# Attention and Mish layer on one core: the scores of pairs 12 to 47 from diagonal steps to side-by-side steps, in seven PSUM banks

## The chip, the core and the metric

The kernel runs on one core of a Trainium2 chip. The core has five engines that run side by side and meet only at semaphores: PE (matrix products, with a weight load, PEld, ahead of each), DVE (vector operations), ACT (activation functions), POOL (further element-wise work) and SP (which here only issues DMAs). PE writes its results to PSUM, eight banks of 128 partitions by 512 fp32 numbers; DVE and ACT read them from there. The metric is the device time of one execution in microseconds (us); lower is better.

## What is computed

For 8 batches of 12 heads, 448 positions and a head dimension of 64, attention with an extra term in the denominator; then, over the 3584 rows of 768 numbers that come out, a layer with Mish between two products (`moe_w_in` is 768 x 2048, `moe_w_out` 2048 x 768).

```python
scores = scale * np.matmul(q, k.transpose(0, 1, 3, 2))
m = np.max(scores, axis=-1, keepdims=True)
e = np.exp(scores - m)
attn = e / (np.sum(e, axis=-1, keepdims=True) + np.exp(-m) + 1e-09)
attn_out = np.matmul(attn, v)
x = attn_out.transpose(0, 2, 1, 3).reshape(B * S, H * D)
h = x @ w_in
sp = np.where(h > 20.0, h, np.log1p(np.exp(np.minimum(h, 20.0))))
out = (h * np.tanh(sp)) @ w_out
```

## The kernel before

Two heads make a **pair**, with their 64-row halves of q and k stacked on 128 partitions; there are 48 pairs, 6 to a batch. Three pairs make a **unit** (`UNIT_PAIRS`), two units a batch. The first six pairs run in a head loop of their own (L548); from unit 2 on, one loop (L575) does for each unit u two stages, one after the other:

- The **step stage** (loop over n, L586): 12 steps, four per pair. A step is one [128 query rows] x [448 keys] block for each of two heads; the fourth step of a pair is one block only, 64 rows of each head. For a step, PE computes scores (`scores`), DVE takes the negated row maxima (L293) and ACT the exponentials with row sums (`exps`, L306). Between the steps stands the other product, `mm2_part`: gT times w_out for rows of a batch that was finished earlier, accumulated over 16 matmuls of 384 columns (a half part) or 192 (a quarter part), in chunks of two matmuls; the list `plan` says which parts run in which unit, 7 quarters in each, 5 in unit 4, the first that has any. When a part is complete, DVE copies it to SBUF (L459) and SP stores it when its row block is complete. `av_pair` (L382) multiplies the transposed exponentials with v, for the pairs of the unit before, into a bank from which DVE casts to xT (L391).
- The **w_in stage** (loop over f, L626): `mm1_mish` eight times, six matmuls of 448 columns each (L406), then ACT's Mish (L412). Between them PE transposes q and k of the next three pairs (L193, at f 1, 3 and 5), `evac_qk` scales q into qT (DVE) and copies k (ACT), and the exponentials of the unit are normalised (two pairs on DVE, L341, the third on POOL, L339) and transposed by DMA on SP's queue (L345). At f 7 the first three steps of the next unit's scores are issued. Mish and exponential use different tables on ACT, so a table is loaded at both ends of the stage; the dummy activation of L649 loads the second ahead of need.

The order on every engine is that of the program (`tc.manual_schedule`); an instruction that waits holds up everything behind it on its engine. `flush_late` issues the copies out of PSUM that earlier calls left in `late`.

PSUM before: three tiles `sc0` to `sc2` of two banks each, used as a ring by step number, and two banks `mo0` and `mo1`, handed out and returned through `mo_free`. Up to three steps are in flight; each step's scores go to PE right behind the step whose exponentials free a tile (`scores_ahead`).

How the scores are formed, from pair 12 (`DIAG_FROM`) on: the first pair of a unit is done side by side, two matmuls that each use 64 of PE's 128 rows (L272, L275), and its fourth step as one full matmul with a block-diagonal q of 64 + 64 rows (`q_rest`, L280). The second and third pair are **diagonal** (`is_diag`): `evac_qk` writes q in seven blocks of 64 rows per head with zeros between (`q_diag`, two scalings L227), and each of the seven blocks is one full 128-row matmul (L266), two per step. `av_pair` of the unit before stands ahead of the fourth step of each pair, in the unused second bank of that step's tile (`av_with`). `gather_mid` (L422) copies, after the second unit of a batch, the 64 rows that are left over at a batch border.

Of the kernel before, what the change touches and what calls it, by code (L numbers as in the profile page):

```python
# [10 lines left out]
BF16 = mybir.dt.bfloat16  # L11
AF = mybir.ActivationFunctionType
ALU = mybir.AluOpType
# [6 lines left out]
def kernel(  # L20
# [70 lines left out]
    for t_ in en_bufs:  # L91
# [10 lines left out]
    def is_diag(p):  # L102
        return p >= DIAG_FROM and p % UNIT_PAIRS > 0

    q_rest = singles.tile([128, 2, 64], BF16)
    nc.gpsimd.memset(q_rest, 0.0)

    loaded, casted, qkT, att, xT, gT, o_sbs, stats = {}, {}, {}, {}, {}, {}, {}, {}
    av_with, mids = {}, {}
    late = deque()  # L110

    def flush_late():
# [88 lines left out]
    def evac_qk(p, act=False):  # L201
        if p >= N_PAIRS:
            return
        (q_ps, k_ps), own = qkT[p]
        mo_free.extend(own)
        qd = q_diag[p % 3]
        kT = qk_pool.tile([128, S], BF16, tag="kT", name="kT")
        if not is_diag(p):
            qT = qd.rearrange("d i h r -> d (i h r)")[:, 0:S]
            qkT[p] = (qT, kT)  # L210
            if act:
                nc.scalar.mul(qT, q_ps[:, 0:S], SCALE)
            else:
                nc.vector.tensor_scalar(
                    out=qT, in0=q_ps[:, 0:S], scalar1=SCALE, scalar2=None, op0=ALU.mult
                )
            if p >= DIAG_FROM:
                nc.gpsimd.tensor_copy(out=q_rest[0:64, 0, :], in_=qT[0:64, 384:S])
                nc.gpsimd.tensor_copy(out=q_rest[64:128, 1, :], in_=qT[64:128, 0:64])
        else:  # L220
            qkT[p] = (qd, kT)
            if p < DIAG_FROM + 3:
                nc.vector.memset(qd[0:64, :, 1, :], 0.0)
                nc.vector.memset(qd[64:128, :, 0, :], 0.0)
            for h in range(2):
                rows = slice(64 * h, 64 * h + 64)
                nc.vector.tensor_scalar(  # L227
                    out=qd[rows, :, h, :],
                    in0=q_ps[rows, 0:S].rearrange("d (i r) -> d i r", i=QB),
                    scalar1=SCALE, scalar2=None, op0=ALU.mult,  # L230
                )
# [14 lines left out]
    def scores(idx):  # L246

        p, s = divmod(idx, STEPS)
        if s == 0:
            if p < HP or p % UNIT_PAIRS == 0:  # L250
                for nm in ("negm", "sums", "expm", "den", "rden"):
                    stats[nm] = st_pool.tile([128, UNIT_PAIRS, NTILE], FP32, tag=nm, name=nm)
            at = 0 if p < HP else p % UNIT_PAIRS
            att[p] = {nm: t[:, at, :] for nm, t in stats.items()}
            att[p].update(en=en_bufs[p % N_EN], whole=dict(stats))
        st = att[p]
        qT, kT = qkT[p]
        kA, kB = kT[0:64, :], kT[64:128, :]
        sc = sc_tiles[idx % len(sc_tiles)]
        if s == STEPS - 1 and p in av_with:  # L260
            av_pair(av_with.pop(p), bank=sc[:, 1, :])
        if is_diag(p):
            cols = tuple(range(2 * s, min(2 * s + 2, NTILE)))
            negm = st["negm"][:, cols[0] : cols[-1] + 1]
            for bk, i in enumerate(cols):
                nc.tensor.matmul(  # L266
                    sc[:, bk, 0:S], lhsT=qT[:, i].rearrange("d h r -> d (h r)"), rhs=kT,
                    start=True, stop=True,
                )
        elif s < 3:  # L270
            qa, qb = 128 * s, 64 + 128 * s
            nc.tensor.matmul(  # L272
                sc[:, 0, 0:S], lhsT=qT[0:64, qa : qa + 128], rhs=kA, start=True, stop=True
            )
            nc.tensor.matmul(  # L275
                sc[:, 1, 0:S], lhsT=qT[64:128, qb : qb + 128], rhs=kB, start=True, stop=True
            )
            cols, negm = (s, 4 + s), st["negm"][:, s : s + 5 : 4]
        elif p >= DIAG_FROM:
            nc.tensor.matmul(  # L280
                sc[:, 0, 0:S], lhsT=q_rest.rearrange("d h r -> d (h r)"), rhs=kT,
                start=True, stop=True,
            )
# [9 lines left out]
        nc.vector.tensor_reduce(  # L293
            out=negm, in_=sc[:, 0 : len(cols), 0:S], axis=AX.X, op=ALU.max, negate=True
        )
        st["sc", s] = (sc, cols)
# [71 lines left out]
    def av_pair(p, act=False, bank=None):  # L368
# [5 lines left out]
        av = mo_take() if bank is None else bank  # L374
        for j in range(NT):
            for h in range(2):
                if is_diag(p):
                    by_h = eT[0:SP_, j, :].rearrange("c (i h r) -> c h i r", h=2, r=64)
                    e_h = by_h[:, h]
                else:  # L380
                    e_h = eT[0:SP_, j, h * S : (h + 1) * S]
                nc.tensor.matmul(  # L382
                    av[h * 64 : (h + 1) * 64, 0:S],
                    lhsT=v_bf[:, h, j * D : (j + 1) * D],
                    rhs=e_h,
                    start=(j == 0), stop=(j == NT - 1),
                )
# [8 lines left out]
        del att[p], casted[p], qkT[p]  # L396


    def mm1_mish(b, ff):
# [3 lines left out]
        spare = ff % FF_U == 1  # L403
        h_ps = sc_tiles[0][:, 0, :] if spare else mo_take()
        for dm in range(DM_T):
            nc.tensor.matmul(  # L406
                h_ps[:, 0:S],
                lhsT=w_in_sb[:, dm, ff * 128 : (ff + 1) * 128],
                rhs=xT[b][:, dm, :],
                start=(dm == 0), stop=(dm == DM_T - 1),  # L410
            )
        nc.scalar.activation(out=gT[b][:, ff, :], in_=h_ps[:, 0:S], func=AF.Mish)  # L412
        if not spare:
            mo_free.append(h_ps)

    def gather_mid(b):
# [75 lines left out]
    plan = {}  # L492
    for g in range(B // 2):
        u0 = first_mm2 + 4 * g
        rest = plan.pop(u0, [])
        if g == 0:
            plan[u0] = [(0, i, 0, 2) for i in range(2)] + [(0, 2, 0, 1)]
            plan[u0 + 1] = [(0, 2, 1, 1)] + [(0, i, 2, 2) for i in range(3)]
# [11 lines left out]
    weight = [5.2] + [1.0] * (steps - STEPS) + [0.4] * (STEPS - 1)  # L510

    BY_POOL = 4
    LEAD = UNIT_PAIRS + 1
# [61 lines left out]
    for u in range(UNITS_PER_B, N_UNITS + 2 * UNITS_PER_B):  # L575
# [6 lines left out]
        if attn and u >= first_mm2:  # L582
            av_with.update({p0 + i: p0 + i - UNIT_PAIRS for i in range(UNIT_PAIRS)})
        end = min((u + 1) * UNIT_PAIRS, N_PAIRS) * STEPS

        for n in range(steps):  # L586
# [3 lines left out]
            if late_tp:  # L590
                transpose_pair(p0 + 2)
            exps(idx)
            if late_tp:
                evac_qk(p0 + 2)
            if u == UNITS_PER_B + 1:
# [27 lines left out]
        b, w = (u - UNITS_PER_B) // UNITS_PER_B, u % UNITS_PER_B  # L623
        nxt = p0 + UNIT_PAIRS
        todo = sorted(range(p0, nxt), key=lambda p: p in BY_PE)
        for f in range(FF_U):  # L626
            if moe:
                mm1_mish(b, w * FF_U + f)
            if u == UNITS_PER_B and f in (2, 6):
                load_w(1)  # L630
            if not attn:
# [7 lines left out]
            if nxt < DIAG_FROM and f in (4, 6):  # L639
                scores_ahead(nxt * STEPS + f // 2 - 1)  # L640
            if f == FF_U - 1:
                scores_ahead(min(nxt * STEPS + 3, N_PAIRS * STEPS))
            if f == 3:
                normalise(todo[1], dma=todo[1] not in BY_PE)
            if f == 4:
# [2 lines left out]

            nc.scalar.activation(out=one, in_=zero, func=AF.Exp)  # L649
        if moe and w == UNITS_PER_B - 1:  # L650
            gather_mid(b)
    flush_late()
    assert not pieces and all(have == 4 for _, have in o_sbs.values())

# [29 lines left out]
```

## Time and profile before

| | us |
|---|---|
| median of three runs | 481.56 (480.86 to 481.75) |
| the profiled execution | 479.95 |
| span of its instructions | 478.0 |
| w_in stage of unit 4 begins (first L406) | 117.73 |
| w_in stage of unit 9 begins | 248.63 |
| w_in stage of unit 10 begins | 274.62 |
| w_in stage of unit 15 begins | 404.79 |

The profiled execution's 479.95 us has the span of 478.0 in it and 1.95 around it. From unit 5 on a unit takes 26.0 us (26.16 in units 8 and 12, 26.66 in unit 6). The span falls into a head (to about 92 us), the units, and a tail from 407 on in which only the two products are left. Four rows of the second part of the page:

```profile
DVE  4888987968787886878687878788787869420021
ACT  5979678878787888979787878888897978412300
POOL 4877809255514334353535242433535340300000
PEclk9998798899999999999999999999999999999999
```

Each digit is the busy share of a fortieth of the span in tenths; in the last row it is the granted PE clock. Times of instructions in the text are from the span's start.

### The profile page before, as it was taken

How to read it: one execution, taken by the hardware profiler on the slowest of the kernel's cores; microseconds unless marked ns; L12 is line 12 of the kernel's file. 1: busy time of each engine (PE TensorE's matmuls, PEld its weight loads, DVE VectorE, ACT ScalarE, POOL GpSimd, SP SyncE). 2: the span in 40 equal slices, each digit the busy share in tenths (PEclk: the TensorE clock that was granted, in tenths of full speed). 3: DMA queues.
4: the chain of work that ended last, by engine and by line, in shares of the span. 5: the costliest groups of instructions: out<-in, count | busy, mean ns of one | idle time of the engine just before them, and what ended most of it. 6: DMA issues, size and time to landing. Idle time of an engine off the chain costs nothing.

```text
span 478.0 us, 8924 instructions
## 1 busy us (share of the span) xinstructions
PE 443.1 (93%) x3064; PEld 248.6 (52%) x3064; DVE 339.1 (71%) x680; ACT 350.0 (73%) x919; POOL 181.1 (38%) x315
## 2 busy tenths in 40 slices
PE   4565888898999999999999999999999999999997
PEld 2233544454655555555555555556555555556565
DVE  4888987968787886878687878788787869420021
ACT  5979678878787888979787878888897978412300
POOL 4877809255514334353535242433535340300000
PEclk9998798899999999999999999999999999999999
DMA  8999969999999989899999999899989595870113
GB/s 228 220 233 220 235 100 234 162 187 238 207 217 276 206 212 219 213 203 246 193 250 182 225 167 228 211 207 234 201 233 212 156 178 127 135 164 24 43 28 105
DMA packets 202381, 90.37 MB, mean 189 GB/s; under 512 B 159072, under 2 KB 198880, under 8 KB 202336
## 3 DMA queue, kind: packets, MB, share of 16 engines
q1 hardware_dynamic: 194848, 83.51, 81.3%
q0 software_dynamic: 7488, 6.29, 8.6%
q8 instruction: 24, 0.39, 0.3%
q14 instruction: 21, 0.17, 0.1%
HBM read 45.61 MB, written 11.01 MB: 118 GB/s over the span
## 4 chain that ended last, share of the span: by engine, by line
PE 76%; ACT 10%; DVE 9%; issue 2%; DMA 1%; POOL 0%; SPq 0%; DVEq 0%; ACTq 0%; POOLq 0%
PE mo L472 26%; PE mo L406 25%; ACT en L306 9%; PE sc L382 6%; DVE negm L293 6%; PE sc L266 5%; PE sc L406 4%; PE sc L193 3%; PE sc L272 2%; PE mo L356 1%; PE mo L382 1%; DVE en L341 1%; PE sc L280 1%; DVE eT L360 1%; DMA k_f<-in_k_dram 1%
## 5 line engine op out<-in xcount | busy, mean ns | idle before, releaser
L306 ACT ACTIVATE en<-sc,negm 128x448 bf16<-128x448 f32 x336 | 209.6, 637 | 26.4 <-DVE xT L391 10.4
L293 DVE TENSOR_REDUCE negm<-sc 128x2 f32<-128x896 f32 x192 | 180.7, 968 | 55.8 <-PE sc L275 26.0
L472 PE MATMUL mo<-w_out_sb,gT 128*128 128x384 bf16 (+1 forms) x912 | 142.3, 301 | 0.0
L406 PE MATMUL mo<-xT,w_in_sb 128*128 128x448 bf16 x672 | 137.7, 353 | 0.6 <-DVE xT L391 0.6
L412 ACT ACTIVATE gT<-mo 128x448 bf16<-128x448 f32 x112 | 61.3, 547 | 68.2 <-PE mo L406 68.1
L472 PEld LDWEIGHTS <-gT 128*128 128x128 bf16 x912 | 84.1, 98 | 48.2 <-issue 5.7
L339 POOL TENSOR_SCALAR en<-en,rden 128x448 bf16<-128x448 bf16 x122 | 76.4, 646 | 80.7 <-DVE rden L331 76.9
L406 PEld LDWEIGHTS <-w_in_sb 128*128 128x128 bf16 x768 | 72.9, 98 | 64.0 <-issue 3.0
L306 ACT ACTIVATION_READ_ACCUMULATOR en<-sc,negm 128x1 f32 x336 | 69.3, 206 | 0.0
L175 POOL CAST q_bf<-q_f 112x512 bf16<-112x512 f32 x47 | 29.0, 617 | 98.4 <-DMA q_f<-in_q_dram 98.0
L341 DVE TENSOR_SCALAR en<-en,rden 128x448 bf16<-128x448 bf16 x214 | 58.6, 345 | 0.9
L459 DVE COPY o_sb<-mo 128x384 f32<-128x384 f32 (+1 forms) x65 | 32.2, 495 | 35.1 <-PE mo L472 34.8
L266 PE MATMUL sc<-kT,qd 128*128 128x448 bf16 x168 | 47.7, 354 | 0.3 <-ACT en L306 0.2
L272 PE MATMUL sc<-kT,qd 64*128 64x448 bf16 x72 | 25.1, 411 | 12.7 <-ACT en L306 11.1
L382 PE MATMUL sc<-eT,v_bf 112*64 112x448 bf16 x288 | 34.1, 357 | 1.9 <-ACT en L306 1.7
L162 POOL CAST v_bf<-v_f 112x512 bf16<-112x512 f32 x48 | 29.5, 616 | 9.7 <-DMA v_f<-in_v_dram 8.8
L382 PEld LDWEIGHTS <-v_bf 112*64 112x64 bf16 x384 | 21.0, 112 | 22.8 <-issue 13.6
L176 POOL CAST k_bf<-k_f 112x512 bf16<-112x512 f32 x47 | 28.9, 616 | 7.5 <-DMA k_f<-in_k_dram 7.0
L227 DVE TENSOR_SCALAR qd<-sc 64x448 bf16<-64x448 bf16 x48 | 18.7, 389 | 11.9 <-PE sc L193 11.2
L266 PEld LDWEIGHTS <-qd 128*128 128x128 bf16 x168 | 16.3, 97 | 18.0 <-issue 9.2
L275 PE MATMUL sc<-kT,qd 64*128 64x448 bf16 x72 | 25.4, 415 | 0.0
L472 PE MATMUL mo<-w_out_sb,mid 128*128 128x384 bf16 x128 | 24.9, 326 | 0.0
(57 smaller groups left out, 340.1 us busy)
## 6 DMA issues: line engine op xcount, KB each, us to landing
q_f<-in_q_dram SPq DMA_DIRECT2D x48, 224.0 KB, 5.1
k_f<-in_k_dram SPq DMA_DIRECT2D x48, 224.0 KB, 5.4
v_f<-in_v_dram SPq DMA_DIRECT2D x48, 224.0 KB, 5.7
w_in_sb<-in_moe_w_in_dram POOLq DMA_DIRECT2D x12, 256.0 KB, 6.1
w_out_sb<-in_moe_w_out_dram POOLq DMA_DIRECT2D x8, 384.0 KB, 7.6
out_dram<-o_sb SPq DMA_DIRECT2D x7, 336.0 KB, 3.3
out_dram<-o_sb SPq DMA_DIRECT2D x8, 288.0 KB, 4.6
out_dram<-o_sb SPq DMA_DIRECT2D x8, 240.0 KB, 2.9
```

Source lines behind the costliest of these rows:

```text
L162: nc.gpsimd.tensor_copy(out=casted[p][2], in_=loaded.pop(p)[2])
L266: nc.tensor.matmul(sc[:, bk, 0:S], lhsT=qT[:, i].rearrange("d h r -> d (h r)"), rhs=kT, start=True, stop=True,)
L272: nc.tensor.matmul(sc[:, 0, 0:S], lhsT=qT[0:64, qa : qa + 128], rhs=kA, start=True, stop=True)
L293: nc.vector.tensor_reduce(out=negm, in_=sc[:, 0 : len(cols), 0:S], axis=AX.X, op=ALU.max, negate=True)
L306: nc.scalar.activation(out=st["en"][:, :, c, 0:SP_], in_=sc[:, bk, 0:S].rearrange("q (j c) -> q j c", j=NT), func=AF.Exp, bias=st["negm"][ ...
L339: nc.gpsimd.tensor_scalar(scalar2=1.0, op0=ALU.mult, op1=ALU.mult, **args)
L341: nc.vector.tensor_scalar(scalar2=None, op0=ALU.mult, **args)
L382: nc.tensor.matmul(av[h * 64 : (h + 1) * 64, 0:S], lhsT=v_bf[:, h, j * D : (j + 1) * D], rhs=e_h, start=(j == 0), stop=(j == NT - 1),)
L406: nc.tensor.matmul(h_ps[:, 0:S], lhsT=w_in_sb[:, dm, ff * 128 : (ff + 1) * 128], rhs=xT[b][:, dm, :], start=(dm == 0), stop=(dm == DM_T - 1),)
L412: nc.scalar.activation(out=gT[b][:, ff, :], in_=h_ps[:, 0:S], func=AF.Mish)
L459: nc.vector.tensor_copy(out=o_sb[:, cols], in_=st["o"][:, 0:n_cols])
L472: nc.tensor.matmul(st["o"][:, 0:n_cols], lhsT=src[:, ff, c0 : c0 + 128], rhs=w_out_sb[:, ff, cols], start=(ff == 0), stop=(ff == FF_T - 1),)
```

## The change

From pair 12 on (`GROUP_FROM`):

- All three pairs of a unit form their scores side by side; `q_diag`, its zeros and its pairs of scalings go. Each pair has its own `q_rest` block (`q_rests`), filled by POOL for all three.
- The ring goes. Step s of a pair has a fixed place: steps 0 to 2 in sc0 to sc2, step 3 in `mo1` (`last_sc`). `mo1` leaves `mo_free`, so that the w_out product has `mo0` alone.
- The order of the step stage is written out (`GROUPED`, one list for even and one for odd units): after the exponentials of step n, so many chunks of the product, the scores of the steps named, or an `av_pair`. Scores of a pair's fourth step and of the next pair's first two are issued together; the third step of a pair goes by itself, ahead of an `av_pair` in most places. `av_pair` uses mo1, or in odd units for the third pair a bank of sc0.
- `plan` is re-cut so that each unit has four parts: half, half, quarter, half.
- The w_in stage takes its banks in a fixed order from sc0, mo0 and mo1 (`MISH_BANK`), and `gather_mid` moves to f 6 of the next unit.

The tail and the units before unit 4 keep their order but for `plan` and `gather_mid`.

```diff
-    QB = S // 64
-    DIAG_FROM = 2 * HP
-    q_diag = [
-        singles.tile([128, QB, 2, 64], BF16, tag=f"qd{i}", name=f"qd{i}") for i in range(3)
+    GROUP_FROM = 2 * HP
+    last_sc = mo_tiles[1].rearrange("p (o n) -> p o n", o=1)
+    q_rests = [
+        singles.tile([128, 2, 64], BF16, tag=f"qr{i}", name=f"qr{i}") for i in range(UNIT_PAIRS)
     ]
...
+        if p >= GROUP_FROM:
+            q_rest = q_rests[p % UNIT_PAIRS]
+            nc.gpsimd.tensor_copy(out=q_rest[0:64, 0, :], in_=qT[0:64, 384:S])
+            nc.gpsimd.tensor_copy(out=q_rest[64:128, 1, :], in_=qT[64:128, 0:64])
...
-        if s == STEPS - 1 and p in av_with:
-            av_pair(av_with.pop(p), bank=sc[:, 1, :])
-        if is_diag(p):
-            cols = tuple(range(2 * s, min(2 * s + 2, NTILE)))
-            negm = st["negm"][:, cols[0] : cols[-1] + 1]
-            for bk, i in enumerate(cols):
-                nc.tensor.matmul(
-                    sc[:, bk, 0:S], lhsT=qT[:, i].rearrange("d h r -> d (h r)"), rhs=kT,
-                    start=True, stop=True,
-                )
-        elif s < 3:
+        if p >= GROUP_FROM:
+            sc = sc_tiles[s] if s < len(sc_tiles) else last_sc
+        if s < 3:
...
         else:
-            plan[u0] = rest + whole(g, 0) + [(g, 1, 0, 1)]
-            plan[u0 + 1] = [(g, 1, 1, 1), (g, 1, 2, 2)] + whole(g, 2)
-        plan[u0 + 2] = [(g, 4, 0, 2), (g, 4, 2, 1)] + whole(g, 3)
-        plan[u0 + 3] = [(g, 4, 3, 1)] + whole(g, 5) + [(g, 6, 0, 2)]
+            plan[u0] = plan.pop(u0) + [(g, 0, 0, 2), (g, 1, 0, 1), (g, 0, 2, 2)]
+            plan[u0 + 1] = [(g, 1, 2, 2), (g, 2, 0, 2), (g, 1, 1, 1), (g, 2, 2, 2)]
+        plan[u0 + 2] = [(g, 4, 0, 2), (g, 4, 2, 2), (g, 5, 0, 1), (g, 5, 1, 2)]
+        plan[u0 + 3] = [(g, 3, 0, 2), (g, 3, 2, 2), (g, 5, 3, 1), (g, 6, 0, 2)]
...
+    GROUPED = (
+        (
+            [("fill", 6), ("av", 0)],
+            [("fill", 2), ("sc", (3, 4, 5))],
+            [("fill", 4)],
+            [("sc", (6,)), ("av", 1)],
+            [("fill", 2)],
+            [("fill", 2), ("sc", (7, 8, 9))],
+            [("fill", 4)],
+            [("fill", 4), ("sc", (10,)), ("av", 2)],
+            [("fill", 3)],
+            [("fill", 2), ("sc", (11,))],
+            [("fill", 3)],
+            [],
+        ),
+        (
+            [("fill", 5)],
+            [("fill", 3), ("sc", (3, 4, 5))],
+            [("fill", 4)],
+            [("sc", (6,)), ("av", 0)],
+            [("fill", 2)],
+            [("fill", 2), ("sc", (7, 8, 9))],
+            [("fill", 4)],
+            [("fill", 4), ("sc", (10,)), ("av", 1)],
+            [("fill", 3)],
+            [("fill", 2), ("sc", (11,))],
+            [("fill", 1), ("av0", 2)],
+            [("fill", 2)],
+        ),
+    )
+    MISH_BANK = (0, 1, 2, 0, 1, 2, 1, 2)
...
             exps(idx)
+            if grouped:
+                flush_late()
+                for what, arg in GROUPED[u % 2][n]:
+                    if what == "fill":
+                        for _ in range(min(arg, len(filler))):
+                            fn, w = filler.popleft()
+                            fn()
+                            done += w
+                    elif what in ("av", "av0"):
+                        bank = mo_tiles[1] if what == "av" else sc_tiles[0][:, 0, :]
+                        av_pair(p0 - UNIT_PAIRS + arg, bank=bank)
+                    else:
+                        flush_late()
+                        for i in arg:
+                            scores(p0 * STEPS + i)
...
+                if to_group:
+                    bank = (sc_tiles[0][:, 0, :], None, mo_tiles[1])[MISH_BANK[f]]
+                mm1_mish(b, w * FF_U + f, bank)
+                if f == 6 and to_gather:
+                    gather_mid(to_gather.popleft())
```

More of the change, by code (lines that the diff above doesn't have):

```diff
@@ L92 @@
         nc.vector.memset(t_[:, :, :, SP_:128], 0.0)
-    QB = S // 64
-    DIAG_FROM = 2 * HP
-    q_diag = [
-        singles.tile([128, QB, 2, 64], BF16, tag=f"qd{i}", name=f"qd{i}") for i in range(3)
-    ]
[L102 to L106, printed above, removed]
+    GROUP_FROM = 2 * HP
+    last_sc = mo_tiles[1].rearrange("p (o n) -> p o n", o=1)
+    q_rests = [
+        singles.tile([128, 2, 64], BF16, tag=f"qr{i}", name=f"qr{i}") for i in range(UNIT_PAIRS)
+    ]
+    for t_ in q_rests:
+        nc.gpsimd.memset(t_, 0.0)
     loaded, casted, qkT, att, xT, gT, o_sbs, stats = {}, {}, {}, {}, {}, {}, {}, {}
-    av_with, mids = {}, {}
+    mids = {}
     late = deque()
@@ L205, in evac_qk @@
         mo_free.extend(own)
-        qd = q_diag[p % 3]
+        qT = qk_pool.tile([128, S], BF16, tag="qT", name="qT")
         kT = qk_pool.tile([128, S], BF16, tag="kT", name="kT")
[L208 to L215, printed above, removed]
-                )
-            if p >= DIAG_FROM:
-                nc.gpsimd.tensor_copy(out=q_rest[0:64, 0, :], in_=qT[0:64, 384:S])
-                nc.gpsimd.tensor_copy(out=q_rest[64:128, 1, :], in_=qT[64:128, 0:64])
-        else:
[L221 to L231, printed above, removed]
+        qkT[p] = (qT, kT)
+        if act:
+            nc.scalar.mul(qT, q_ps[:, 0:S], SCALE)
+        else:
+            nc.vector.tensor_scalar(
+                out=qT, in0=q_ps[:, 0:S], scalar1=SCALE, scalar2=None, op0=ALU.mult
+            )
[3 more added lines that the diff above has]
+            nc.gpsimd.tensor_copy(out=q_rest[64:128, 1, :], in_=qT[64:128, 0:64])
         if p == 0 or own and not act:
@@ L259, in scores @@
         sc = sc_tiles[idx % len(sc_tiles)]
-        if s == STEPS - 1 and p in av_with:
-            av_pair(av_with.pop(p), bank=sc[:, 1, :])
-        if is_diag(p):
-            cols = tuple(range(2 * s, min(2 * s + 2, NTILE)))
-            negm = st["negm"][:, cols[0] : cols[-1] + 1]
-            for bk, i in enumerate(cols):
-                nc.tensor.matmul(
-                    sc[:, bk, 0:S], lhsT=qT[:, i].rearrange("d h r -> d (h r)"), rhs=kT,
-                    start=True, stop=True,
-                )
-        elif s < 3:
+        if p >= GROUP_FROM:
+            sc = sc_tiles[s] if s < len(sc_tiles) else last_sc
+        if s < 3:
             qa, qb = 128 * s, 64 + 128 * s
@@ L278, in scores @@
             cols, negm = (s, 4 + s), st["negm"][:, s : s + 5 : 4]
-        elif p >= DIAG_FROM:
+        elif p >= GROUP_FROM:
             nc.tensor.matmul(
-                sc[:, 0, 0:S], lhsT=q_rest.rearrange("d h r -> d (h r)"), rhs=kT,
+                sc[:, 0, 0:S],
+                lhsT=q_rests[p % UNIT_PAIRS].rearrange("d h r -> d (h r)"), rhs=kT,
                 start=True, stop=True,
@@ L376, in av_pair @@
             for h in range(2):
[L377 to L381, printed above, removed]
+                e_h = eT[0:SP_, j, h * S : (h + 1) * S]
                 nc.tensor.matmul(
@@ L396, in av_pair, with mm1_mish @@
         del att[p], casted[p], qkT[p]
-    def mm1_mish(b, ff):
+    def mm1_mish(b, ff, bank=None):
         if ff == 0:
@@ L402, in mm1_mish @@
         flush_late()
-        spare = ff % FF_U == 1
-        h_ps = sc_tiles[0][:, 0, :] if spare else mo_take()
+        h_ps = mo_take() if bank is None else bank
         for dm in range(DM_T):
@@ L412, in mm1_mish @@
         nc.scalar.activation(out=gT[b][:, ff, :], in_=h_ps[:, 0:S], func=AF.Mish)
-        if not spare:
+        if bank is None:
             mo_free.append(h_ps)
@@ L494 @@
         u0 = first_mm2 + 4 * g
-        rest = plan.pop(u0, [])
         if g == 0:
-            plan[u0] = [(0, i, 0, 2) for i in range(2)] + [(0, 2, 0, 1)]
-            plan[u0 + 1] = [(0, 2, 1, 1)] + [(0, i, 2, 2) for i in range(3)]
-        else:
-            plan[u0] = rest + whole(g, 0) + [(g, 1, 0, 1)]
-            plan[u0 + 1] = [(g, 1, 1, 1), (g, 1, 2, 2)] + whole(g, 2)
-        plan[u0 + 2] = [(g, 4, 0, 2), (g, 4, 2, 1)] + whole(g, 3)
-        plan[u0 + 3] = [(g, 4, 3, 1)] + whole(g, 5) + [(g, 6, 0, 2)]
+            plan[u0] = [(0, 0, 0, 2), (0, 1, 0, 2), (0, 2, 0, 1)]
+            plan[u0 + 1] = [(0, 0, 2, 2), (0, 1, 2, 2), (0, 2, 1, 1), (0, 2, 2, 2)]
+        else:
+            plan[u0] = plan.pop(u0) + [(g, 0, 0, 2), (g, 1, 0, 1), (g, 0, 2, 2)]
+            plan[u0 + 1] = [(g, 1, 2, 2), (g, 2, 0, 2), (g, 1, 1, 1), (g, 2, 2, 2)]
+        plan[u0 + 2] = [(g, 4, 0, 2), (g, 4, 2, 2), (g, 5, 0, 1), (g, 5, 1, 2)]
+        plan[u0 + 3] = [(g, 3, 0, 2), (g, 3, 2, 2), (g, 5, 3, 1), (g, 6, 0, 2)]
         if g < B // 2 - 1:
@@ L510 @@
     weight = [5.2] + [1.0] * (steps - STEPS) + [0.4] * (STEPS - 1)
+    GROUPED = (
[27 more added lines that the diff above has]
+        ),
+    )
+    MISH_BANK = (0, 1, 2, 0, 1, 2, 1, 2)
+    to_gather = deque()
     BY_POOL = 4
@@ L581 @@
         p0 = u * UNIT_PAIRS
-        if attn and u >= first_mm2:
-            av_with.update({p0 + i: p0 + i - UNIT_PAIRS for i in range(UNIT_PAIRS)})
+        grouped = attn and p0 >= GROUP_FROM
+        if u == N_UNITS:
+            mo_free.append(mo_tiles[1])
         end = min((u + 1) * UNIT_PAIRS, N_PAIRS) * STEPS
@@ L592 @@
             exps(idx)
+            if grouped:
[13 more added lines that the diff above has]
+                            scores(p0 * STEPS + i)
+                if n in LOAD_AT:
+                    load_pair(p0 + LOAD_AT.index(n) + LEAD)
+                    cast_pair(p0 + LOAD_AT.index(n) + LEAD - 1)
+                if u - UNITS_PER_B < len(W_AT):
+                    load_w(W_AT[u - UNITS_PER_B].get(n, 0))
+                continue
             if late_tp:
@@ L625 @@
         todo = sorted(range(p0, nxt), key=lambda p: p in BY_PE)
+        to_group = attn and nxt >= GROUP_FROM
+        if to_group and nxt == GROUP_FROM:
+            flush_late()
+            mo_free.remove(mo_tiles[1])
+            rg["next"] = N_PAIRS * STEPS
         for f in range(FF_U):
             if moe:
-                mm1_mish(b, w * FF_U + f)
+                bank = sc_tiles[0][:, 0, :] if f == 1 else None
+                if to_group:
[3 more added lines that the diff above has]
+                    gather_mid(to_gather.popleft())
             if u == UNITS_PER_B and f in (2, 6):
@@ L638 @@
                 evac_qk(nxt + f // 2)
-            if nxt < DIAG_FROM and f in (4, 6):
+            if not to_group and f in (4, 6):
                 scores_ahead(nxt * STEPS + f // 2 - 1)
-            if f == FF_U - 1:
-                scores_ahead(min(nxt * STEPS + 3, N_PAIRS * STEPS))
+            if f == FF_U - 1 and not to_group:
+                scores_ahead(nxt * STEPS + 3)
+            if f == FF_U - 1 and to_group and nxt < N_PAIRS:
+                for s in range(3):
+                    scores(nxt * STEPS + s)
             if f == 3:
@@ L650 @@
         if moe and w == UNITS_PER_B - 1:
-            gather_mid(b)
+            to_gather.append(b)
+            if u == N_UNITS + UNITS_PER_B - 1:
+                gather_mid(to_gather.popleft())
     flush_late()
```

## The prediction

> **What bounds the kernel now.** I read the page first, then stage by stage one period of the steady part, engine by engine, and last the few places where an engine was seen to wait.
>
> ```profile
> PE 443.1 (93%) x3064; PEld 248.6 (52%) x3064; DVE 339.1 (71%) x680; ACT 350.0 (73%) x919; POOL 181.1 (38%) x315
> PE 76%; ACT 10%; DVE 9%; issue 2%; DMA 1%; POOL 0%; SPq 0%; DVEq 0%; ACTq 0%; POOLq 0%
> 259.74:274.79 15.05, 15.05 (x104) 8.52 (x105) 13.46 (x19) 13.56 (x40) 6.04 (x11) 1.00 1.11 220
> ```
>
> The first two lines are the page's busy time and its chain by engine; the third is a window over the step stage of one unit: length, then busy time of PE, PEld, DVE, ACT, POOL, granted clock, DMA. PE has no hole, at full clock; DVE and ACT have about 1.5 us left each. So PE is the bound, but nothing near it is idle. The starts of the first matmul of L406 in neighbouring units lie 26.0 us apart, and that period is what the change can move, in the 12 units from pair 12 on.
>
> The PE timeline of that unit, and under it one place of an earlier unit:
>
> ```profile
> 256.63 2.44 PE L406 MATMUL mo<-xT,w_in_sb 128*128 128x448 bf16 x12
> 259.00 0.36 PE L272 MATMUL sc<-kT,qd 64*128 64x448 bf16 x1
> 259.00 0.36 PE L275 MATMUL sc<-kT,qd 64*128 64x448 bf16 x1
> ...
> 259.67 3.44 PE L472 MATMUL mo<-w_out_sb,gT 128*128 128x384 bf16 x24
> 263.04 0.95 PE L382 MATMUL sc<-eT,v_bf 112*64 112x448 bf16 x8
> 263.92 0.36 PE L280 MATMUL sc<-kT,q_rest 128*128 128x448 bf16 x1
> 264.11 0.82 PE L472 MATMUL mo<-w_out_sb,gT 128*128 128x192 bf16 x8
> 264.77 0.54 PE L266 MATMUL sc<-kT,qd 128*128 128x448 bf16 x2
> 265.15 0.81 PE L472 MATMUL mo<-w_out_sb,mid 128*128 128x384 bf16 x4
> 265.80 0.54 PE L266 MATMUL sc<-kT,qd 128*128 128x448 bf16 x2
> ```
>
> ```profile
> 68.84 1.30 PE L406 MATMUL mo<-xT,w_in_sb 128*128 128x448 bf16 x6
> 70.07 0.36 PE L272 MATMUL sc<-kT,qd 64*128 64x448 bf16 x1
> ...
> 70.37 1.31 PE L406 MATMUL mo<-xT,w_in_sb 128*128 128x448 bf16 x6
> ```
>
> Starts, not lengths, give PE's pace: 0.65 us for four 384-wide matmuls (0.1625 each), 0.66 for eight 192-wide ones (0.0825), 0.19 for a 448-wide one. A diagonal step is two of these in a row, 0.38. A side-by-side step runs both heads at once (259.00 twice) and costs 0.19 in a row, but going in and out costs too: L406 ends at 68.84 + 6 x 0.19 = 69.98, the step starts at 70.07 and the next work at 70.37, so 0.09 in and 0.11 out, 0.39 for a lone step. Three in a row took 258.90 (256.63 + 2.27) to 259.67, 0.77. The L382 block, 0.98 with its two gaps, has the same.
>
> The Trainium skill, "TensorEngine Tiling (Array Packing)", promises up to 2x for a contract dimension of 64 (Overview) and says that changing the tiling mode drains the engine (Tiling Modes, Key Properties); the gaps of 0.09 and 0.11 agree with the drain. By the 2x alone, the sum would be the free-switch figure that stands with the rivals.
>
> **PE's work, part by part.** Per unit, before: 0.77 + 15 x 0.19 + 3 x 0.98 = 6.56 us for scores and L382. After: 0.77 for steps 0 to 2; twice a full 64+64 step and two side by side, 0.19 + 0.58 = 0.77; twice a lone step with L382 behind it, 0.09 + 0.19 + 0.11 + 0.88 = 1.27; the last full step 0.19; the third L382 0.98. Sum 6.02, a gain of 0.54 per unit, 6.5 us over 12 units. The w_out product is 7 quarters in both, 9.12.
>
> **The waits it adds.** One bank (mo0) holds the product, so each of the four parts (half, half, quarter, half) must be copied out by L459's copy before the next starts. Bounds from rows:
>
> ```profile
> 62.73 0.61 DVE L391 CAST xT<-mo 128x448 bf16<-128x448 f32 x1
> 63.40 1.41 PE L406 MATMUL mo<-xT,w_in_sb 128*128 128x448 bf16 x6 [0.58 <-DVE xT L391]
> 264.38 0.62 DVE L293 TENSOR_REDUCE negm<-sc 128x1 f32<-128x448 f32 x1 [0.76 <-PE sc L280]
> 259.10 0.54 ACT L412 ACTIVATE gT<-mo 128x448 bf16<-128x448 f32 x1 [0.59 <-PE mo L406]
> 259.66 1.28 ACT L649 ACT_TABLE_LOAD   x1
> 261.06 0.62 ACT L306 ACTIVATE en<-sc,negm 128x448 bf16<-128x448 f32 x1
> 262.89 0.64 ACT L306 ACTIVATE en<-sc,negm 128x448 bf16<-128x448 f32 x1
> ```
>
> DVE's end reaches PE 0.06 later (63.34 to 63.40); PE's last issue reaches DVE 0.27 later (264.11 to 264.38). A half part's hand-over is 0.27 + 0.55 + 0.06 = 0.88 if DVE is free, and a reduction of 1.0 longer at worst, when the copy just misses; the score group between covers 0.77. I take DVE's own queue, written out below.
>
> Count from the end of the L406 stage (258.90 = 0). ACT's first exponential starts at 2.16: the last L412, a table load of 1.28 and the small activation stand before it, and the diff leaves them. The fourth starts at 3.99, and PE may reuse its bank 0.76 later (as 87.50 to 88.27, L286), at 4.75. DVE needs 1.0 per two-bank reduction, 0.55 per one-bank, 0.52 for xT, 0.46 or 0.27 for a product copy.
>
> Even units (L382 of the first pair at once):
> - PE: 12 matmuls to 2.72, L382 2.83 to 3.71, part one ends 4.36. Copy 4.63, bank free 5.24. Steps 3, 4, 5 end at 5.12: 0.12 lost.
> - Step 6 and L382 to 7.81, part two ends 9.11. DVE has been full (reductions 3 to 6, then xT, 5.09 to 9.16), so step 7 waits for xT until 9.31 (0.2 lost); steps 7 to 9 end at 10.07.
> - Quarter ends 11.39. Its copy stands behind reductions 7, 8, 9 and runs at 12.39; bank free 12.80, PE ready at 12.66 after step 10 and L382: 0.14 lost.
> - 2.6 of product and 0.19: the L406 stage starts at 15.59. Before: 274.62 - 258.90 = 15.72. Gain 0.13.
>
> Odd units (no L382 before the first group):
> - Part one ends at 3.37. Step 4's bank is free in time; step 5 stands until 4.75: 0.93 lost, with all PE work queued behind it.
> - Part two ends 8.94, copy 9.21, bank free 9.82 (0.12 lost; step 6's L382 0.1 more). Reductions 7 to 9 end 12.22, quarter's bank free 12.63 against 12.41: 0.22 lost. Then 2.6 + 0.19 + 0.98: 16.40. Loss 0.69.
>
> Unit 4 has only five quarters, and its product is not what fills it: before 117.73 - 102.12 = 15.61, after the same table without part four, bounded by xT at 14.33 and step 11: 14.52. Gain 1.1.
>
> **What I cost at nothing.** POOL: six q_rest copies instead of two, 4 x 0.24 = 1.0 us; POOL is busy 10 of 26, and the last pair's stand behind a 4.33 us normalise, pushing the casts by 0.5; these are needed a stage later (uncovered: 0.5 per unit). DVE: L227's two scalings of 0.39 become one per pair, 0.8 us less in the L406 stage, where DVE idles anyway. The mid copy (0.75) moves from 262.40 into that stage; between the last q scaling (257.5) and the first reduction (259.40) it fits (uncovered: 0.75 every second unit). SP's queue keeps its transposes and loads; the transposes issued at 252.79 and landing 6.2 to 8.1 later are there by 2.0, before the even L382 at 2.83 (a late one would delay that unit alone). ACT ends its exponentials at about 16.2, 0.6 after the L406 stage began (before: 1.3); its third block there needs them only at 2.7.
>
> **Sum.** Unit 4: -1.1. Odd 5 to 15: 6 x 0.69 = +4.1. Even 6 to 14: 5 x -0.13 = -0.65, and units 8 and 12 took 26.16 before, -0.3. Together +2.1: 479.95 of the profiled execution (span 478.0 and 1.95 around it) becomes 482.0, and by the median 481.56 + 2.1 = 483.7. I call 0.2% (1 us) what a measurement can tell.
>
> **Rivals.**
> - The odd wait doesn't bind, and odd units run like even ones: 11 x -0.13 - 1.1 - 0.3 = -2.8, 478.8, faster. It decides once ACT frees step 1's bank 0.9 sooner than 4.75; nothing in the diff moves ACT's start, which speaks against it. With hand-overs hidden too, PE's sum alone: -6.5 and unit 4's 0.5, about 474.5. With free switches, 0.19 x 6 = 1.1 per unit, 468; the gaps at 70.07 and 70.37 speak against that. Together 0.25, mostly the first.
> - A product copy slips behind one more reduction on DVE, whose queue in my table has only 0.2 us of air from 5 to 14: 1.0 per unit, 6 us more if in one kind of unit (489.7), 12 if in both (495.7). It needs steps 3 to 6 some 0.3 later than I have them. 0.2.
> - What the mode switches give and what the hand-overs take cancel: 481.6. This needs half of my odd loss. 0.1.
> - My forecast, 480.5 to 487 by itself: 0.45.
>
> The range 477 to 491 leaves out the far ends of both sides. Faster 0.27, same 0.13, slower 0.6 follow from these, with the forecast's own lower edge on both sides of the bound.
>
> **What would show it.** PE idle of about 0.9 per odd unit before the side-by-side matmul of step 5, released by ACT; short idles before L472's product released by DVE's copy; starts of the L406 stage about 25.9 and 26.7 apart in turn; reductions back to back on DVE. I am wrong if the PE gaps stay under 0.3 per unit, or if step 5 finds its bank free, or if the copies wait a whole reduction.

## The result and the profile after

The changed kernel takes 482.63 us (median of 9 runs, 482.16 to 484.31) against 480.86 us (479.85 to 481.78) before: a ratio of 1.0045, 95% interval 1.0032 to 1.0058. It is slower, by 1.8 us in the medians. The profiled execution of the changed kernel took 483.19 us with a span of 481.1.

The page of the changed kernel, its busy times and its chain:

```profile
PE 439.6 (91%) x3064; PEld 237.6 (49%) x3064; DVE 328.9 (68%) x652; ACT 348.7 (72%) x919; POOL 193.9 (40%) x365
...
PE 72%; DVE 14%; ACT 6%; issue 4%; DMA 3%; POOL 0%; DVEq 0%; SPq 0%; ACTq 0%; POOLq 0%
```

PE works 3.5 us less (439.6 against 443.1) in a span that is 3.1 us longer, and DVE's share of the chain rises from 9 to 14%: work was saved on PE, and waits took more than that. (Line numbers shift with the change: L406 is now L377, L412 is L383, L472 is L443, L382 is L354, L293 is L269, L306 is L282, L459 is L430, L391 is L363, L339 is L315, L649 is L689; L280 is L255, L272 and L275 are L247 and L250.)

The periods of the units, from the first matmul of the w_in stage of the unit before to that of the unit, as read from the PE timelines of the profiled executions:

| unit | 4 | 5 | 6 | 7 | 8 | 9 | 10 | 11 to 15 |
|---|---|---|---|---|---|---|---|---|
| before | 26.31 | 26.08 | 26.66 | 26.01 | 26.16 | 26.00 | 26.00 | 26.00, 26.16, 26.00, 25.99, 26.01 |
| after | 24.81 | 27.56 | 27.45 | 26.80 | 25.87 | 26.80 | 25.87 | 26.80, 25.87, 26.80, 25.87, 26.80 |

Even units gain 0.13 (0.29 in 8 and 12), odd units lose 0.80. This is the PE timeline of an odd unit's step stage (11) in the changed kernel:

```profile
286.96 2.77 PE L443 MATMUL mo<-w_out_sb,mid 128*128 128x384 bf16 x16
289.57 0.35 PE L255 MATMUL mo<-kT,qr 128*128 128x448 bf16 x1
289.86 0.36 PE L247 MATMUL sc<-kT,qT 64*128 64x448 bf16 x1
289.86 0.36 PE L250 MATMUL sc<-kT,qT 64*128 64x448 bf16 x1
290.97 0.35 PE L247 MATMUL sc<-kT,qT 64*128 64x448 bf16 x1 [0.75 <-DVE negm L269]
290.97 0.36 PE L250 MATMUL sc<-kT,qT 64*128 64x448 bf16 x1
291.27 1.47 PE L443 MATMUL mo<-w_out_sb,mid 128*128 128x384 bf16 x8
...
301.87 0.82 PE L443 MATMUL mo<-w_out_sb,gT 128*128 128x384 bf16 x4
302.73 1.29 PE L377 MATMUL sc<-xT,w_in_sb 128*128 128x448 bf16 x6
```

The second side-by-side step of the group (step 5) starts 1.11 us after the first where 0.2 is its pace: 0.91 lost, with everything behind it on PE late by that. The view puts the wait down to a reduction on DVE, whose end (290.91) falls together with the real one. ACT's timeline has the other candidate, the last exponential out of the bank that step 5 writes:

```profile
288.36 0.62 ACT L282 ACTIVATE en<-sc,negm 128x448 bf16<-128x448 f32 x1
...
290.19 0.64 ACT L282 ACTIVATE en<-sc,negm 128x448 bf16<-128x448 f32 x1
290.70 0.21 ACT L282 ACTIVATION_READ_ACCUMULATOR en<-sc,negm 128x1 f32 x1
```

The exponential ends at 290.19 + 0.64 = 290.83; the read of its row sum behind it, which in the trace is the operation that signals, ends at 290.91, and PE starts 0.06 later. Reduction and read end together, so this profile cannot tell which of the two it was; an experiment below does. An even unit (10) has no such hole:

```profile
264.02 0.82 PE L443 MATMUL mo<-w_out_sb,gT 128*128 128x384 bf16 x4
264.88 0.35 PE L255 MATMUL mo<-kT,qr 128*128 128x448 bf16 x1
265.16 0.36 PE L247 MATMUL sc<-kT,qT 64*128 64x448 bf16 x1
265.16 0.36 PE L250 MATMUL sc<-kT,qT 64*128 64x448 bf16 x1
265.36 0.35 PE L247 MATMUL sc<-kT,qT 64*128 64x448 bf16 x1
265.36 0.35 PE L250 MATMUL sc<-kT,qT 64*128 64x448 bf16 x1
265.64 1.47 PE L443 MATMUL mo<-w_out_sb,gT 128*128 128x384 bf16 x8
...
272.05 0.95 PE L354 MATMUL mo<-eT,v_bf 112*64 112x448 bf16 x8
273.14 1.79 PE L443 MATMUL mo<-w_out_sb,gT 128*128 128x384 bf16 x10
```

Two steps in a row, 0.20 apart, and the product's next part starts 0.28 after the second, 0.19 for the step and 0.09 for going out: the first hand-over of the product's bank costs nothing here. The quarter's costs 0.21 (272.05 + 0.88 = 272.93 to 273.14). On DVE the same unit shows how little room there is:

```profile
264.20 0.62 DVE L363 CAST xT<-mo 128x448 bf16<-128x448 f32 x1 [0.29 <-PE mo L354]
264.88 0.56 DVE L430 COPY o_sb<-mo 128x384 f32<-128x384 f32 x1
265.36 0.61 DVE L269 TENSOR_REDUCE negm<-mo 128x1 f32<-128x448 f32 x1
265.89 3.08 DVE L269 TENSOR_REDUCE negm<-sc 128x2 f32<-128x896 f32 x3
268.88 0.61 DVE L363 CAST xT<-mo 128x448 bf16<-128x448 f32 x1
269.74 0.56 DVE L430 COPY o_sb<-mo 128x384 f32<-128x384 f32 x1 [0.24 <-PE mo L443]
270.21 0.61 DVE L269 TENSOR_REDUCE negm<-mo 128x1 f32<-128x448 f32 x1
270.74 2.08 DVE L269 TENSOR_REDUCE negm<-sc 128x2 f32<-128x896 f32 x2
272.74 0.35 DVE L430 COPY o_sb<-mo 128x192 f32<-128x192 f32 x1
```

From the first product copy to the quarter's, DVE has one idle time of 0.24 us. The first row costs PE something else: step 3 (L255) writes mo1, the bank that this cast reads. The product ends at 264.02 + 4 x 0.1625 = 264.67, the cast at 264.82, and step 3 starts at 264.88, 0.21 late.

### The profile page after: what moved, and what is told of

Read it like the earlier page. It is cut to its first block, busy times and chain, and to the rows that moved or that the text cites. A ratio compares the mean times of both kernels' runs of the same rounds, so it can differ in the third digit from the quotient of the medians.

```text
span 481.1 us, 8897 instructions
## 1 busy us (share of the span) xinstructions
PE 439.6 (91%) x3064; PEld 237.6 (49%) x3064; DVE 328.9 (68%) x652; ACT 348.7 (72%) x919; POOL 193.9 (40%) x365
## 4 chain that ended last, share of the span: by engine, by line
PE 72%; DVE 14%; ACT 6%; issue 4%; DMA 3%; POOL 0%; DVEq 0%; SPq 0%; ACTq 0%; POOLq 0%
PE mo L443 26%; PE mo L377 21%; DVE negm L269 9%; PE sc L377 7%; PE sc L247 5%; PE mo L354 5%; ACT en L282 4%; PE sc L189 3%; DMA eT<-en 2%; DVE o_sb L430 2%; PE mo L332 2%; PE mo L255 1%; DVE en L317 1%; PE sc L354 1%; DMA k_f<-in_k_dram 1%
## 5 line engine op out<-in xcount | busy, mean ns | idle before, releaser
L282 ACT ACTIVATE en<-sc,negm 128x448 bf16<-128x448 f32 x300 | 186.6, 645 | 12.8 <-DVE negm L269 8.9
L269 DVE TENSOR_REDUCE negm<-sc 128x2 f32<-128x896 f32 (+1 forms) x156 | 158.0, 1048 | 37.9 <-PE sc L250 30.7
L443 PE MATMUL mo<-w_out_sb,gT 128*128 128x384 bf16 (+1 forms) x912 | 138.6, 301 | 1.5
L377 PE MATMUL mo<-xT,w_in_sb 128*128 128x448 bf16 x594 | 122.4, 352 | 0.6 <-DVE xT L363 0.6
L443 PEld LDWEIGHTS <-gT 128*128 128x128 bf16 x912 | 81.0, 98 | 58.5 <-issue 23.2
L383 ACT ACTIVATE gT<-mo 128x448 bf16<-128x448 f32 x99 | 53.9, 545 | 72.7 <-PE mo L377 72.7
L377 PEld LDWEIGHTS <-w_in_sb 128*128 128x128 bf16 x768 | 72.8, 98 | 66.5 <-issue 5.3
L315 POOL TENSOR_SCALAR en<-en,rden 128x448 bf16<-128x448 bf16 x122 | 77.7, 654 | 58.1 <-DVE rden L307 54.2
L430 DVE COPY o_sb<-mo 128x384 f32<-128x384 f32 (+1 forms) x65 | 32.5, 500 | 48.8 <-PE mo L443 47.6
L282 ACT ACTIVATION_READ_ACCUMULATOR en<-sc,negm 128x1 f32 x300 | 65.1, 217 | 0.0
L247 PE MATMUL sc<-kT,qT 64*128 64x448 bf16 x144 | 48.3, 386 | 17.2 <-ACT en L282 11.3
L250 PE MATMUL sc<-kT,qT 64*128 64x448 bf16 x144 | 48.6, 389 | 0.0
L354 PE MATMUL mo<-eT,v_bf 112*64 112x448 bf16 x336 | 41.0, 368 | 2.4 <-DMA eT<-en 1.5
L377 PE MATMUL sc<-xT,w_in_sb 128*128 128x448 bf16 x174 | 37.6, 352 | 0.2
L208 DVE TENSOR_SCALAR qT<-sc 128x448 bf16<-128x448 bf16 x39 | 15.2, 389 | 27.6 <-PE sc L189 27.6
L213 POOL COPY qr<-qT 64x64 bf16<-64x64 bf16 x36 | 8.8, 245 | 56.3 <-DVE qT L208 56.2
L354 PEld LDWEIGHTS <-v_bf 112*64 112x64 bf16 x384 | 18.6, 111 | 21.7 <-issue 11.9
L363 DVE CAST xT<-mo 128x448 bf16<-128x448 f32 x39 | 24.0, 617 | 7.2 <-PE mo L354 7.2
```

The source lines that it names most:

```text
L247: nc.tensor.matmul(sc[:, 0, 0:S], lhsT=qT[0:64, qa : qa + 128], rhs=kA, start=True, stop=True)
L250: nc.tensor.matmul(sc[:, 1, 0:S], lhsT=qT[64:128, qb : qb + 128], rhs=kB, start=True, stop=True)
L269: nc.vector.tensor_reduce(out=negm, in_=sc[:, 0 : len(cols), 0:S], axis=AX.X, op=ALU.max, negate=True)
L282: nc.scalar.activation(out=st["en"][:, :, c, 0:SP_], in_=sc[:, bk, 0:S].rearrange("q (j c) -> q j c", j=NT), func=AF.Exp, bias=st["negm"][ ...
L315: nc.gpsimd.tensor_scalar(scalar2=1.0, op0=ALU.mult, op1=ALU.mult, **args)
L354: nc.tensor.matmul(av[h * 64 : (h + 1) * 64, 0:S], lhsT=v_bf[:, h, j * D : (j + 1) * D], rhs=e_h, start=(j == 0), stop=(j == NT - 1),)
```

## The experiments

**The odd list replaced by the even one.** If the odd loss is PE standing at step 5, putting `av_pair` ahead of the first group must end it. The whole list is exchanged, so the other two `av_pair` come earlier as well; the experiment on ACT's tables below keeps the order and changes only when ACT starts.

```diff
-                for what, arg in GROUPED[u % 2][n]:
+                for what, arg in GROUPED[1 if u == 5 else 0][n]:
```

> The changed kernel, with the list of the even units in every unit but 5, so that units 7, 9, 11, 13 and 15 put the first pair's L354 ahead of the first score group. Theory (the odd loss is PE standing at step 5 for the bank that ACT still reads): these five units fall from 26.80 to the 25.87 of the even ones, 5 x 0.93 = 4.65 us less than the changed kernel, about 478.0, below the kernel before. Rival (one product bank and DVE's queue cost the same whatever stands in front): odd units stay near 26.8 and the time near 482.6.

Units 7 to 15 have periods of 25.87 or 25.88 each, and the view of waits names none on PE from unit 7 on (by the starts, waits like those of the even unit above remain). The time is 478.92 us, a ratio of 0.9978 (0.9961 to 0.9995) to the kernel before. That is faster than the kernel before, though only just, and 0.67%, 3.2 us, below the changed kernel's ratio, where 4.65 was expected. In the profiled execution unit 6 took 2.1 us more than in the changed kernel; its windows (length, then busy time of PE, PEld, DVE, ACT, POOL, granted clock, DMA) and its PE timeline:

```profile
155.40:157.90 2.50, 0.30 (x4) 0.08 (x4) 0.93 (x1) 2.50 (x10) 2.15 (x6) 1.00 1.29 211
157.90:161.70 3.80, 3.80 (x17) 1.08 (x17) 1.59 (x3) 0.79 (x4) 0.00 (x0) 0.55 1.05 224
```

```profile
153.51 2.12 PE L443 MATMUL mo<-w_out_sb,gT 128*128 128x384 bf16 x12
157.82 1.48 PE L354 MATMUL mo<-eT,v_bf 112*64 112x448 bf16 x8 [2.19 <-DMA eT<-en]
```

PE stood from 155.46 (12 matmuls from 153.51) to 157.82 for transposed exponentials that landed at 157.78, and then worked at a mean granted clock of 0.55 for 3.8 us (0.50 from 158.10 to 161.51). Unit 6 took 29.53 us, against 27.45 in the changed kernel, where the stand was 156.11 to 157.80 and the clock stayed at 1.00.

**Unit 6 with the odd list as well.**

```diff
-                for what, arg in GROUPED[u % 2][n]:
+                for what, arg in GROUPED[1 if u in (5, 6) else 0][n]:
```

> As the one before, but unit 6, too, takes the list of the odd units, since its transposed exponentials land late (157.75, 161.06 and 165.74 in the profile, 4.4, 7.7 and 12.3 us after the L377 stage ended) and the even list asks for them at 2.8, 6.9 and 11.8. Theory (unit 6 stands for that landing): its 27.45 becomes about 26.7, 0.7 us less than the other, about 477.3. Rival (unit 6 is long for another reason): same as the other or slower.

477.25 us, ratio 0.9954 (0.9934 to 0.9975), against 0.9978 for the other on the same chip; unit 6 has 26.80, as expected. The medians lie 1.7 us apart where 0.7 was expected, and the intervals overlap; the slow clock in unit 6 of the other version would account for the rest, if most of its executions have it, which was not measured. (The profiled execution of this kernel is its slowest, 482.41 us: units 2 and 3, which this change doesn't touch, begin 3.5 to 3.8 us later, and unit 5 took 28.48 against 26.79, for a reason that the last section gives; from unit 7 on its periods are 25.87 and 25.88.) This version is faster than both kernels.

**No change of tables on ACT.** Exp takes the place of Mish, so the layer computes another function.

```diff
-        nc.scalar.activation(out=gT[b][:, ff, :], in_=h_ps[:, 0:S], func=AF.Mish)
+        nc.scalar.activation(out=gT[b][:, ff, :], in_=h_ps[:, 0:S], func=AF.Exp)
```

> The changed kernel with Exp in place of Mish in L383, so that ACT never changes its table: the layer computes another function, all else stays. ACT's first exponential of a unit then starts about 1.3 us earlier. Theory (odd units lose because ACT frees step 1's bank at 4.75): the bank is free at about 3.5, the idle time before step 5 goes, odd units fall from 26.8 to about 26.0, even units stay at 25.9 within 0.1: 5 us less, about 477.7. Rival (the odd loss is the hand-over of the product bank): odd units stay near 26.8.

Odd units have 26.33, even ones 25.87; 479.51 us, ratio 0.9993 (0.9973 to 1.0013). ACT's timeline of an odd unit (11), PE's, and the reduction on DVE:

```profile
284.90 0.63 ACT L282 ACTIVATE en<-sc,negm 128x448 bf16<-128x448 f32 x1 [0.85 <-POOL en L315]
...
286.74 0.64 ACT L282 ACTIVATE en<-sc,negm 128x448 bf16<-128x448 f32 x1
287.26 0.21 ACT L282 ACTIVATION_READ_ACCUMULATOR en<-sc,negm 128x1 f32 x1
```

```profile
286.88 0.36 PE L247 MATMUL sc<-kT,qT 64*128 64x448 bf16 x1
...
287.52 0.35 PE L247 MATMUL sc<-kT,qT 64*128 64x448 bf16 x1 [0.28 <-ACT en L282]
```

```profile
287.33 0.61 DVE L269 TENSOR_REDUCE negm<-mo 128x1 f32<-128x448 f32 x1
```

The expectation was right in kind and too large in size. ACT did not start 1.3 us earlier: the first exponential waits until 284.90, 0.1 behind the end of the first row maxima on DVE (283.72 + 1.08; the view names a normalisation on POOL, whose pieces end at 284.35 and 284.97, not there), so it starts 1.68 after the w_in stage ended (283.22) and not 2.16. These 0.48 us come back as 0.47 in each odd unit and as nothing in an even one. And it settles the releaser: step 5 starts 0.05 after the end of ACT's read (287.47), while the reduction that the view named for the changed kernel stands on DVE from 287.33 to 287.94 here and is not waited for.

**Side by side alone, one step at a time**, in the ring, with both product banks:

```diff
     def is_diag(p):
-        return p >= DIAG_FROM and p % UNIT_PAIRS > 0
+        return False
...
-    q_rest = singles.tile([128, 2, 64], BF16)
-    nc.gpsimd.memset(q_rest, 0.0)
+    q_rests = [
+        singles.tile([128, 2, 64], BF16, tag=f"qr{i}", name=f"qr{i}") for i in range(UNIT_PAIRS)
+    ]
+    for t_ in q_rests:
+        nc.gpsimd.memset(t_, 0.0)
```

> The kernel before with one part of the change alone: all pairs from 12 on side by side, each with its own q_rest block, in the ring of three tiles as before, so that each side-by-side step of the second and third pair goes by itself between chunks of the product; two product banks, order and plan as before. Theory (going in and out of side-by-side costs 0.09 and 0.11): a lone step costs 0.39 against 0.38 of a diagonal one, six per unit, 0.1 us per unit slower, 1 us in all: no difference that shows, 480 to 483. Rival (the two heads side by side halve a step's PE time wherever it stands): 6 x 0.19 = 1.1 per unit, 13.5 us faster, 467.

481.22 us, ratio 1.0020 (1.0007 to 1.0033), 1 us; the steady periods are 26.10 where they were 26.00. One lone step on PE's timeline (L472 is L476 in this kernel, L272 and L275 are L276 and L279):

```profile
317.11 0.81 PE L476 MATMUL mo<-w_out_sb,gT 128*128 128x384 bf16 x4
317.86 0.36 PE L276 MATMUL sc<-kT,qd 64*128 64x448 bf16 x1
317.86 0.36 PE L279 MATMUL sc<-kT,qd 64*128 64x448 bf16 x1
318.15 0.82 PE L476 MATMUL mo<-w_out_sb,gT 128*128 128x384 bf16 x4
```

317.11 + 0.65 is 317.76: 0.39 from the end of one chunk to the start of the next, against 0.38 for a diagonal step. Of the halved matmul time nothing is left when a step stands alone; the grouping is what the change lives from. The four added copies on POOL and the missing scalings on DVE are in this run too; all three together come to 0.1 us per unit.

**One bank alone**, in the kernel before:

```diff
+        one_bank = attn and u >= first_mm2
+        if one_bank:
+            flush_late()
+            mo_free.remove(mo_tiles[1])
         for n in range(steps):
...
         assert done == total
+        if one_bank:
+            mo_free.append(mo_tiles[1])
```

> The kernel before with the other part of the change alone: in the step stage of units 4 to 15 the product has one bank instead of two, its order and the diagonal steps as they were. Theory (a hand-over of the bank costs 0.88 us where DVE is free, and a reduction of 1.0 us more where the copy stands behind one; the changed kernel hides it under its score groups): three hand-overs in a unit, the first with nothing in between, the others behind one diagonal step of 0.38 whose reduction goes ahead of the copy, 0.9 + 1.5 + 1.5 = 4 us per unit, at least 1.5 where they fall well; periods of 27.5 to 30 us, 498 to 528. Rival (the hand-over is hidden behind the scores wherever they stand, and the order written out adds nothing): periods stay within 0.2 of 26.0, 480 to 483.

541.20 us (two runs), ratio 1.1264 (1.1213 to 1.1315), 60 us slower, past the upper end of what was expected; steady periods alternate between 30.95 and 31.58. DVE's timeline at the first hand-over, and PE's:

```profile
291.83 0.75 DVE L422 COPY mid<-gT 128x1024 bf16<-128x1024 bf16 x1
292.50 0.54 DVE L459 COPY o_sb<-mo 128x384 f32<-128x384 f32 x1
```

```profile
289.09 2.77 PE L472 MATMUL mo<-w_out_sb,gT 128*128 128x384 bf16 x16
293.09 0.82 PE L472 MATMUL mo<-w_out_sb,gT 128*128 128x192 bf16 x8 [1.23 <-DVE o_sb L459]
...
295.58 0.54 PE L266 MATMUL sc<-kT,qd 128*128 128x448 bf16 x2
297.66 0.81 PE L472 MATMUL mo<-w_out_sb,mid 128*128 128x384 bf16 x4 [1.53 <-DVE o_sb L459]
```

Sixteen matmuls end at 291.69 and the bank is free at 293.09: 1.40, 0.88 of it the bare hand-over and 0.52 the mid copy that stands in front on DVE. The next costs 1.70 (two matmuls from 295.58 end at 295.96) and the third 1.91. Together 5.0 us in this unit (10), where I expected 4: I had left the mid copy out of the first, and at the later ones three operations stand in front of the copy, a one-block reduction, the cast to xT and a two-block reduction, not one reduction. The units with 31.58 have no mid copy, but there the first part is a quarter, and its copy stands behind the reductions of steps 0 to 2: 1.82, and 1.91 for each of the others, 5.6 together. The changed kernel pays for its hand-overs 0.25 us in an even unit (0.04 at the second, 0.21 at the quarter's).

**xT of the second pair on ACT**, in the version with the odd list in units 5 and 6 and the even one elsewhere:

```diff
-                        av_pair(p0 - UNIT_PAIRS + arg, bank=bank)
+                        av_pair(
+                            p0 - UNIT_PAIRS + arg, bank=bank,
+                            act=arg == 1 and u not in (5, 6),
+                        )
```

> The version with the even list in every unit but 5 and 6, and in it the second pair's xT copied by ACT (a copy of 0.54 us) instead of DVE (0.52 in the queue). Theory (in the even list PE still stands some 0.3 us per unit at the hand-overs because DVE's queue is full from the first copy to the last reduction, and ACT has room): the copies come up to 0.5 earlier, the hand-over of the quarter part costs 0.2 less, periods fall from 25.87 to about 25.65, 1.5 to 2 us in all, about 475.5. Rival (ACT has no room: exponentials 0.5 later free the score banks later): periods of 25.9 or more, 477.3 or above.

477.24 us, ratio 0.9937 (0.9915 to 0.9959), and periods of 25.87 and 25.88, as without it: neither the gain nor a loss. On PE's timeline of an even unit the wait for the quarter's copy shrinks from 0.21 to 0.08 (L354 at 269.04, done 0.88 later, next work at 270.00), and step 9 starts 0.14 later than its pace, since ACT's copy delays the exponentials that free its bank. What one queue gives the other takes.

The new `plan`, the fixed banks of the w_in stage and the later `gather_mid` were not run by themselves.

## Why the prediction came out

- **PE's work.** The forecast took a lone step at 0.39, two in a row at 0.58, and 0.54 us saved per unit. The lone step alone in the ring confirmed the first (26.10 against 26.00, an expected 0.1), the even timeline the second (265.16 to 265.64, with 0.10 before it). The Trainium skill, "TensorEngine Tiling (Array Packing)", Tiling Modes, says that a change of tiling mode drains the engine; the lone step agrees with it, and the speedup of up to twofold of its Overview did not appear where steps stand alone.
- **Even units.** Forecast 15.59 for the step stage against 15.72; measured periods 25.87 against 26.00, 0.13 less, which is the forecast. The waits come to 0.46 in both, but not in the same places, so that the agreement to the hundredth is partly luck. Forecast were 0.12 and 0.14 at two hand-overs and 0.2 for xT at step 7. In unit 10 the first hand-over costs nothing, the second 0.04, the quarter's 0.21; step 7 does not wait, and step 3 waits 0.21 for the first pair's xT. The forecast reckoned with the bank mo1, which `av_pair` and a pair's fourth step share, at step 7 and not at step 3.
- **Odd units.** Forecast 0.93 lost at step 5 and 0.69 in sum; measured 0.91 and 0.80. The missing 0.1 is mostly at the end: the w_in stage waits for the third pair's xT, and the forecast put no wait there. Its cast starts 1.06 after the first matmul of L354 (300.99 to 302.05) and ends at 302.67, so L377 starts at 302.73, 0.2 behind the product's end. The second hand-over costs 0.05 and not 0.12. (The forecast's 0.1 for the L354 behind step 6 is not in its own sum, and no such wait shows: 292.67 to 292.97.) That the wait at step 5 is what odd units lose was shown from both sides: another order ends it (25.87), and ACT's earlier start shortens it by as much as it is earlier (0.48 and 0.47).
- **Units 4 to 6.** The step stage of unit 4 took 14.53 us (its w_in stage starts 115.56, the one before ended 101.03), forecast 14.52. In this execution 0.76 of that went again in its w_in stage, where one small operation on DVE (L295, the softmax denominators) took 1.17 us where 0.18 is usual; why is not known. Unit 6, forecast to gain 0.13, lost 0.79: PE stood 1.69 us for the transposed exponentials, which landed at 157.75. I had priced a late landing at that unit alone and not put it into the sum; the range of 6.2 to 8.1 us that I used was of one later unit. The trace of the kernel before already has 8.54 for the transpose in this place (149.12 to 157.66), the changed kernel 9.14. Why it lands late here stays open: the last weights had landed by 128.90.
- **The sum.** In the profiles: 0.67 less up to unit 3, which the change doesn't touch, unit 4 -1.50, unit 5 +1.48, unit 6 +0.79, odd units from 7 +3.98, even ones -0.83, tail -0.20: +3.1. Forecast was +2.1, the medians differ by 1.8. Three of these parts are not the change's: the 0.67; 0.42 of unit 4's 1.50, which lies in unit 3's w_in stage (in the profile before, it began at a granted clock of 0.50, from 91.42 to 92.32); and the 0.76 in unit 5. Without them the profiles have +3.4. Of the 1.3 above the forecast, 0.9 are unit 6 and 0.6 the odd units; the tail gives 0.2 back. So the loss per odd unit and its place were right, and that the medians came so near to the forecast is partly luck: the execution profiled before lies 0.9 below its median, the one after 0.6 above, and where the others differ is not known.
- **The rivals.** That odd units run like even ones would have made the kernel faster, and the first experiment shows that this rival was right about the price (25.87) and wrong about the condition: nothing in the change itself moved ACT. The copy one reduction later did not happen in the changed kernel; the single bank in the old order shows what copies cost that stand behind several operations, 5.0 to 5.6 us per unit. That gains and hand-overs cancel needed half of the odd loss, which came in full (0.80).

## What to carry to other kernels

A change of tiling mode has an entry and an exit price, here 0.09 and 0.11 us; half-array matmuls of 448 columns paid only in groups, so work out a group's length before trading banks for it. Giving up a double buffer was cheap where enough other work of the same engine stood at each hand-over and little stood in front of the copy: 0.25 us per even unit with an order written out, 5.0 to 5.6 without. When such an order is written for two kinds of iteration, follow each from the first release of the engine that starts late; the missing block of 1 us ahead of a wait was most of the difference between a loss of 0.45% and a gain of 0.46%; the rest is unit 6.

## What was not expected

A stand of PE of 2.36 us in unit 6 was followed by 3.8 us at a granted clock of 0.55, one of 1.69 us in the same place by none. The length alone does not decide it. Ahead of unit 4's w_in stage PE waits for an xT in both versions of the first two experiments, equally long, and the third row is a window behind the wait in the second of them:

```profile
115.49 0.35 PE L255 MATMUL mo<-kT,qr 128*128 128x448 bf16 x1 [1.66 <-DVE xT L363]
119.01 0.35 PE L255 MATMUL mo<-kT,qr 128*128 128x448 bf16 x1 [1.66 <-DVE xT L363]
119.42:122.83 3.41, 3.41 (x11) 1.41 (x10) 2.44 (x6) 3.26 (x7) 2.92 (x5) 0.50 1.18 237
```

In the first version the clock stayed at 1.00 (115.67 to 125.94); in the second it was 0.50 for 3.41 us, which loses 1.7, and unit 5 took 28.48 against 26.79. In the kernel with one bank a stand of 2.07 us (to 237.21) was followed by none. The Trainium skill, "TensorE: Matmul & The Clock Gate", HAM oscillation, warns of idle gaps of more than about 3.4 us; shorter gaps were enough here, in two executions. So a wait that looks like 2 us can cost 3.7 (29.53 against 25.87 for that unit). What decides it, and in how many executions it happens, was not measured.
